# Attention and a gated feed-forward on one core: row sums moved to other slots, feed-forward from an earlier pair, and feed-forward steps in 32-column tiles

## The chip, the core and the metric

The kernel runs on one core of a Trainium2 chip. The core has a matrix engine (TensorE, PE in the profile, its weight loads PEld), a vector engine (VectorE, DVE), an engine for functions such as exp and tanh (ScalarE, ACT), a general engine (GpSimd, POOL) and a queue engine (SyncE, SP), which work side by side and wait for each other by semaphores. DMA engines move data between main memory (HBM) and the on-chip memory SBUF. TensorE writes its results to a second on-chip memory, PSUM, from which VectorE or ScalarE must fetch them.

The metric is the device time of one execution, in microseconds. Before the change it is 474.34 us (median of three runs, 473.15 to 475.47).

## The reference

```python
# q, k, v: (8, 12, 448, 64) float32       batch, heads, sequence, head size
scores = matmul(q, k^T) / sqrt(64)
attn   = exp(scores - max(scores)); attn = attn / (sum(attn) + 1e-9)
x      = matmul(attn, v)                  # then heads side by side: (3584, 768)
g      = x @ w_gate                       # (768, 1536)
val    = x @ w_val                        # (768, 1536)
out    = (g * sigmoid(g) * val) @ w_out   # (1536, 768) -> (3584, 768) float32
```

So there is attention for 96 heads, and then a gated feed-forward block over the 3,584 tokens. The kernel leaves out the subtraction of the maximum, because the scores are small, and works in 16-bit floats with sums in 32 bits.

## The kernel before

Heads are taken two at a time: 48 pairs, six to a batch. The main loop has one slot for each pair. Each slot has two halves, and in each half TensorE makes half of the pair's scores, which ScalarE turns into exponentials E.

```python
    def qk_half(pr, half):
        ...
        for c in (2 * half, 2 * half + 1):
            s = ps_s.tile([128, 2, 512], FP32, tag="s")          # two buffers
            for hx in range(2):
                nc.tensor.matmul(s[:, hx, 0:S], lhsT=t[ts(hx, 64)]..., rhs=t[ts(hx, 64), NC:, :]..., ...)
            nc.scalar.activation(E[pr][:, c], s[0:P, :, 0:S], AF.Exp, scale=sm_scale)
```

The two matmuls of a chunk use 64 rows of the array each. The product with V ("PV") uses four column tiles of 32 columns, and so do the row sums of E, which two pairs share. PV is copied out of PSUM by VectorE.

```python
    def pv(pr):
        acc = ps_a.tile([128, 512], FP32, tag="acc")             # one buffer
        for c in range(NC):
            for j in range(4):
                nc.tensor.matmul(acc[ts(j, 32), 0:S], lhsT=vt[:, 2 * r + j // 2, c, ts(j % 2, 32)],
                                 rhs=E[pr][:, c, j // 2, :], ...)
        xr = attp.tile([128, S], FP32, tag="xraw")
        nc.vector.tensor_copy(xr[:], acc[:, 0:S])

    def sum_rows(p0, acc):
        for c in range(NC):
            for j in range(4):
                nc.tensor.matmul(acc[ts(j, 32), 0:S], lhsT=ones[:], rhs=E[p0 + j // 2][:, c, j % 2, :], ...)
```

For batch 0 the reciprocal sums are spread over the 64 rows of each head by a float32 matmul with a selector matrix, and VectorE multiplies PV with them into X, the input of the feed-forward. For later batches DMAs spread them instead, and GpSimd multiplies.

```python
    def sums_pe(p0, pieces):
        acc = ps_f.tile([128, 512], FP32, tag="f")
        sum_rows(p0, acc)
        R = attp.tile([128, S], FP32, tag="R", bufs=2)
        for lo, hi in pieces:
            nc.vector.reciprocal(R[:, lo:hi], acc[:, lo:hi])

        def spread():
            for lo, hi in pieces:
                for u in range(2):
                    rb = ps_f.tile([128, 512], FP32, tag="f", name="rb")
                    nc.tensor.matmul(rb[:, lo:hi], lhsT=sel[:, u, :], rhs=R[:, lo:hi], start=True, stop=True)
                    mult(p0 + u, nc.vector, rb, lo, hi)
        return spread
```

The feed-forward is cut into steps: the gate (gp), the value (vp) and the output (op). Each step is a group of 6 or 12 matmuls of 128 rows by 128 columns.

```python
    def ffn1_steps(kk, c0, n, hts):
        for fb in range(NFB):
            gp = ps_f.tile([128, 512], FP32, tag="f")            # three buffers for f
            for cb in range(NCB):
                nc.tensor.matmul(gp[:, 0:n], lhsT=wslice("g", fb, cb), rhs=X[kk][:, cb, ds(c0, n)], ...)
            ...  # tanh on ScalarE, then vp in the same way, two operations on VectorE
```

The main loop, cut to the order in which a slot issues its work; steps of the feed-forward fill both halves of a slot, up to a budget that spreads a block evenly over the slots until the next one:

```python
        wp = ps_f.tile([128, 512], FP32, tag="f", name="wp")
        for _ in range(7):
            nc.tensor.matmul(wp[:], lhsT=warm[:, 0:128], rhs=warm[:], start=True, stop=True)
        ...
        for pr in range(NPAIR + 1):
            ...
            if pr == NHP:                      # pair 6: end of batch 0
                pv(pr - 1)
                spread = sums_pe(pr - 2, ((0, 192), (192, S)))
            if pr < NPAIR:
                qk_half(pr, 0)
            if pr == 0:
                turn()                         # transposes of pair 1
            ...
            if pr >= 1 and pr != NHP:
                pv(pr - 1)
            if pr > NHP and pr % 2 == 0:
                work, mults = sums(pr - 2)
                ...
            if pr in add_at:                   # from pair FIRST = 7
                add_block(add_at[pr])
            ...
            carry = ffn_run(state["left"] / slots + carry)
            if pr < NPAIR:
                qk_half(pr, 1)
            if turn2:
                turn2()                        # transposes of pair pr + 2
            if pr in (3, 5, 6):
                spread()
            if pr in (2, 4):
                spread = sums_pe(pr - 2, ((0, S),))
            ...
            carry = ffn_run(state["left"] / max(1, slots - 1) + carry)
```

Of the kernel before, what the change touches and what calls it, by code (L numbers as in the profile page):

```python
# [10 lines left out]
FP32 = mybir.dt.float32  # L11
# [7 lines left out]
GP = 3  # L19
NPE = 11  # L20
LA = 6
FIRST = 7


@with_exitstack
def kernel(
# [10 lines left out]
    nc = tc.nc  # L37
    B, H, S, D = q.shape
# [6 lines left out]
    NHP = H // 2  # L45
# [9 lines left out]
            name=nc.get_next_instruction_name(),  # L55
# [132 lines left out]
    def pv(pr):  # L188
        g, r = divmod(pr, GP)
        vt = v16[g]  # L190
        acc = ps_a.tile([128, 512], FP32, tag="acc")
        for c in range(NC):
            for j in range(4):
                nc.tensor.matmul(  # L194
                    acc[ts(j, 32), 0:S],
                    lhsT=vt[:, 2 * r + j // 2, c, ts(j % 2, 32)],
                    rhs=E[pr][:, c, j // 2, :],
                    start=(c == 0),
                    stop=(c == NC - 1),
                )  # L200
        xr = attp.tile([128, S], FP32, tag="xraw")
        nc.vector.tensor_copy(xr[:], acc[:, 0:S])  # L202
        xraw[pr] = xr

    def mult(pr, eng, rb, lo=0, hi=S):
# [19 lines left out]
# [4 lines that stand above are left out]
        for lo, hi in pieces:  # L229
            nc.vector.reciprocal(R[:, lo:hi], acc[:, lo:hi])  # L230

        def spread():
            for lo, hi in pieces:
                for u in range(2):
                    rb = ps_f.tile([128, 512], FP32, tag="f", name="rb")
                    nc.tensor.matmul(  # L236
                        rb[:, lo:hi], lhsT=sel[:, u, :], rhs=R[:, lo:hi], start=True, stop=True
                    )
                    mult(p0 + u, nc.vector, rb, lo, hi)

        return spread

    def sums(p0):
# [18 lines left out]
        work.append(bcast)  # L262
        return work, [lambda u=u: mult(p0 + u, nc.gpsimd, Rb[p0 + u]) for u in range(2)]

    def ffn1_steps(kk, c0, n, hts):
        for fb in range(NFB):
            gp = ps_f.tile([128, 512], FP32, tag="f")
            for cb in range(NCB):
                nc.tensor.matmul(  # L269
                    gp[:, 0:n],  # L270
                    lhsT=wslice("g", fb, cb),
                    rhs=X[kk][:, cb, ds(c0, n)],
                    start=(cb == 0),
                    stop=(cb == NCB - 1),
                )
            sg = fp.tile([128, 512], FP32, tag="sg")
            nc.scalar.activation(sg[:, 0:n], gp[:, 0:n], AF.Tanh, scale=0.5)  # L277
            yield NCB * n / 2400.0
            vp = ps_f.tile([128, 512], FP32, tag="f")
            for cb in range(NCB):  # L280
                nc.tensor.matmul(  # L281
                    vp[:, 0:n],
                    lhsT=wslice("v", fb, cb),
                    rhs=X[kk][:, cb, ds(c0, n)],
                    start=(cb == 0),
                    stop=(cb == NCB - 1),
                )
            t1 = fp.tile([128, 512], FP32, tag="t1")
            nc.vector.scalar_tensor_tensor(  # L289
                t1[:, 0:n], sg[:, 0:n], 1.0, gp[:, 0:n], ALU.add, ALU.mult  # L290
            )
            nc.vector.scalar_tensor_tensor(  # L292
                hts[:, fb, 0:n], t1[:, 0:n], 0.5 * HS, vp[:, 0:n], ALU.mult, ALU.mult
            )
            yield NCB * n / 2400.0

    def ffn2_steps(kk, c0, n, hts, last_block):
        for ch in range(n // 128):
            osb = fp.tile([128, DM], FP32, tag="osb", bufs=2)
            for oh in range(2):  # L300
                if last_block and ch == n // 128 - 1 and oh == 1:
                    osb = fp.tile([128, DM], FP32, tag="osb", bufs=2)
                op = ps_f.tile([128, 512], FP32, tag="f")
                for fb in range(NFB):
                    nc.tensor.matmul(  # L305
                        op[:, 0:OH],
                        lhsT=hts[:, fb, ts(ch, 128)],
                        rhs=wo[fb // (NFB // 3)][:, fb % (NFB // 3), ts(oh, OH)],
                        start=(fb == 0),
                        stop=(fb == NFB - 1),  # L310
                    )
                last = last_block and ch == n // 128 - 1
                if last and oh == 1:
                    m = OH // 2
                    nc.scalar.activation(
                        osb[:, OH : OH + m], op[:, 0:m], AF.Copy, scale=1.0 / HS
                    )
                    nc.vector.tensor_scalar_mul(osb[:, OH + m : DM], op[:, m:OH], 1.0 / HS)
                else:
                    nc.scalar.activation(osb[:, ts(oh, OH)], op[:, 0:OH], AF.Copy, scale=1.0 / HS)  # L320
                if oh == 1 or last:
                    m0, m1 = (oh * OH, oh * OH + OH) if last else (0, DM)
                    l0 = c0 + ch * 128
                    l = l0
                    while l < l0 + 128:
                        b, j = divmod(l, S)
                        c, p0 = divmod(j, P)
                        m = min(P - p0, l0 + 128 - l)
                        eng = nc.scalar if last and m < 64 else nc.sync
                        eng.dma_start(  # L330
                            out[ts(NB * kk + b, S), :].rearrange("(p c) m -> c p m", c=NC)[
                                c, p0 : p0 + m, m0:m1
                            ],
                            osb[l - l0 : l - l0 + m, m0:m1],
                        )
                        l += m
                yield NFB * OH / 2400.0
# [7 lines left out]
    with tc.manual_schedule():  # L345
# [13 lines left out]
        load_qk16(3, 1)  # L359
        load_qk16(4)  # L360
        load_v(1)
        wp = ps_f.tile([128, 512], FP32, tag="f", name="wp")
        for _ in range(7):
            nc.tensor.matmul(wp[:], lhsT=warm[:, 0:128], rhs=warm[:], start=True, stop=True)
        prep(0)()
        turn = prep(1)

# [11 lines left out]
        def emit(item):  # L379
            if item[0] == "qk":  # L380
                load_qk16(*item[1:])
            elif item[0] == "V":
                load_v(item[1])
            else:
                load_w(*item)
# [49 lines left out]
        add_at = {FIRST: 0}  # L435
        for i in range(1, B - 1):
            add_at[NHP * (i + 1) + DELAY] = i
        for pr in range(NPAIR + 1):
            if pr in add_at:
                pop_deferred(99)  # L440
            nxt = min([x for x in add_at if x > pr] + [NPAIR + 4])
            slots = 2 * (nxt - pr)
            turn2 = None
            if NPE <= pr + LA < NPAIR:
                load_qk(pr + LA, touch=pr < 9)
            if pr == NHP:
                pv(pr - 1)
                spread = sums_pe(pr - 2, ((0, 192), (192, S)))
            if pr < NPAIR:
                qk_half(pr, 0)  # L450
            if pr == 0:
                turn()
            if pr + 3 < NPAIR and pr + 3 >= NPE:
                prep(pr + 3)
            if pr + 2 < NPAIR:
                if pr + 2 < NPE:
                    turn2 = prep(pr + 2)
                if (pr + 2) % GP == GP - 1 and 4 <= (pr + 2) // GP + 1 < NGRP:
                    load_v((pr + 2) // GP + 1)
            if pr >= 1 and pr != NHP:  # L460
                pv(pr - 1)
            if pr > NHP and pr % 2 == 0:
                work, mults = sums(pr - 2)
                deferred.extend(work)
                held[pr + 1] = mults
            if pr in add_at:
                add_block(add_at[pr])
            for w in wq.pop(pr, []):
                emit(w)
            carry = ffn_run(state["left"] / slots + carry)  # L470
            if pr < NPAIR:
                qk_half(pr, 1)
            if turn2:
                turn2()
            if pr in (3, 5, 6):
                spread()
            if pr in (2, 4):
                spread = sums_pe(pr - 2, ((0, S),))
            for fn in held.pop(pr, []):
                deferred.append(fn)  # L480
            if not backlog:
                pop_deferred(7)
            carry = ffn_run(state["left"] / max(1, slots - 1) + carry)
        for fns in held.values():
            deferred.extend(fns)
        ffn_run(1e9)
# [35 lines left out]
```

The softmax here doesn't subtract the row's maximum and nothing guards it: scores larger than these inputs give would overflow.

## Time and profile before

| what | value |
|---|---|
| time, median of three | 474.34 us |
| span of the profiled execution | 473.3 us |
| exponentials on ScalarE | 192 of 915 ns, 164.4 us busy |
| gate, value and output matmuls | 576 + 576 + 672 |
| PV and row-sum matmuls | 768 + 384 |
| granted TensorE clock, mean | 0.991 |

A line of the profile's groups names the line of the kernel, the engine, the operation, what is written and read, the tile, and how often. The matmuls on TensorE are pipelined: the profile's length of a matmul includes its way through the array, and the next one starts well before that ends. So what a group costs is read from the start of one group to the start of the next.

### The profile page before, as it was taken

The numbers are of one execution on the slowest core, as the hardware profiler recorded it, in microseconds if no ns is written. First come the engines' busy times: TensorE is split into PE (matmuls) and PEld (weight loads), VectorE is DVE, ScalarE is ACT, GpSimd is POOL, SyncE is SP. The second block draws the span as 40 slices with busy tenths as digits, with TensorE's granted clock in tenths as the row PEclk, the third lists the DMA queues.
The fourth block names the chain that finished last, engine by engine and source line by source line (L and its number), as shares of the span: only waits on it lengthen the run. The fifth ranks groups of instructions, "written<-read, shape, count | busy, mean of one in ns | idle before, by whom it ended". The sixth has DMA issues, their size and how long they took to land.

```text
span 473.3 us, 8811 instructions
## 1 busy us (share of the span) xinstructions
PE 461.7 (98%) x3559; PEld 219.4 (46%) x3559; DVE 245.3 (52%) x383; ACT 237.4 (50%) x345; POOL 120.8 (26%) x164
## 2 busy tenths in 40 slices
PE   7989999999999999999999999999999999999996
PEld 3335444433345545444444554444444445554453
DVE  3676775077665644636555545456365456334310
ACT  5765665555555465454455465455545552222221
POOL 9534032522443044030340340330401111000000
PEclk8999999999999999999999999999999999999999
DMA  9999999986966595645847668754743312201123
GB/s 142 196 209 239 200 231 187 255 167 117 186 150 133 113 194 135 122 110 125 173 100 160 150 155 136 162 118 93 139 87 67 72 40 73 67 1 34 35 66 101
DMA packets 86025, 62.03 MB, mean 131 GB/s; under 512 B 38496, under 2 KB 82528, under 8 KB 85984
## 3 DMA queue, kind: packets, MB, share of 16 engines
q1 hardware_dynamic: 63872, 46.53, 43.3%
q0 software_dynamic: 22048, 14.88, 22.3%
q8 instruction: 28, 0.46, 0.4%
q14 instruction: 13, 0.11, 0.1%
q10 hardware_dynamic: 64, 0.05, 0.0%
HBM read 47.19 MB, written 11.01 MB: 123 GB/s over the span
## 4 chain that ended last, share of the span: by engine, by line
PE 91%; ACT 3%; DMA 3%; issue 1%; SPq 0%; DVE 0%; POOL 0%; ACTq 0%; POOLq 0%
PE gp L269 24%; PE vp L281 24%; PE op L305 21%; PE s L179 9%; PE acc L194 8%; PE acc L217 4%; ACT E L186 3%; PE rb L236 1%; DMA out_dram<-osb 1%; PE tp L164 1%; DMA Rb<-R 1%; DMA rk<-in_k_dram 1%; SPq L153 0%; POOL qk L150 0%; POOL X L210 0%
## 5 line engine op out<-in xcount | busy, mean ns | idle before, releaser
L186 ACT ACTIVATE E<-s 112x896 f16<-112x896 f32 x192 | 164.4, 915 | 33.2 <-PE s L179 33.2
L269 PE MATMUL gp<-X,wg 128*128 128x384 f16 (+1 forms) x576 | 125.1, 353 | 0.0
L281 PE MATMUL vp<-X,wv 128*128 128x384 f16 (+1 forms) x576 | 124.9, 353 | 0.0
L305 PE MATMUL op<-wo,hts 128*128 128x384 f16 x672 | 117.0, 326 | 0.0
L210 POOL TENSOR_TENSOR X<-xr,Rb 128x448 f16<-128x448 f32 x42 | 47.6, 1133 | 259.7 <-DMA Rb<-R 258.5
L277 ACT ACTIVATE sg<-gp 128x384 f32<-128x384 f32 (+1 forms) x96 | 52.3, 544 | 103.1 <-PE gp L269 103.0
L289 DVE SCALAR_TENSOR_TENSOR t<-sg,gp 128x384 f32<-128x384 f32 (+1 forms) x96 | 58.8, 612 | 83.2 <-ACT sg L277 82.5
L305 PEld LDWEIGHTS <-hts 128*128 128x128 f16 x672 | 64.8, 98 | 48.3 <-issue 4.5
L281 PEld LDWEIGHTS <-wv 128*128 128x128 f16 x576 | 54.3, 98 | 57.1 <-issue 8.9
L269 PEld LDWEIGHTS <-wg 128*128 128x128 f16 x576 | 52.6, 98 | 60.3 <-issue 16.7
L292 DVE SCALAR_TENSOR_TENSOR hts<-t,vp 128x384 f16<-128x384 f32 (+1 forms) x96 | 59.6, 621 | 29.8 <-PE vp L281 22.2
L320 ACT ACTIVATE osb<-op 128x384 f32<-128x384 f32 x55 | 27.0, 491 | 93.7 <-PE op L305 90.6
L202 DVE COPY xr<-acc 128x448 f32<-128x448 f32 x48 | 29.7, 619 | 80.8 <-PE acc L194 79.6
L251 DVE RECIPROCAL R<-ssb 128x112 f32<-128x112 f32 x84 | 66.9, 828 | 0.7
L179 PE MATMUL s<-qkT 64*128 64x448 f16 x384 | 55.6, 361 | 5.6 <-ACT E L186 4.4
L194 PE MATMUL acc<-E,vt 112*32 112x448 f16 x768 | 45.9, 360 | 0.0
L179 PEld LDWEIGHTS <-qkT 64*128 64x128 f16 x384 | 12.3, 94 | 41.4 <-issue 37.8
L194 PEld LDWEIGHTS <-vt 112*32 112x32 f16 x768 | 16.3, 96 | 26.0 <-issue 18.3
L150 POOL CAST qk<-rk 112x512 f16<-112x512 f32 x37 | 22.7, 614 | 0.0
L150 POOL CAST qk<-rq 112x512 f16<-112x512 f32 x37 | 22.7, 613 | 0.0
L217 PE MATMUL acc<-E,ones 112*32 112x448 f16 x384 | 22.4, 353 | 0.0
L126 POOL DMA_DIRECT2D vt<-in_v_dram x17 | 13.5, 792 | 2.4 <-DMA wg<-in_moe_w_gate_dram 2.4
(37 smaller groups left out, 94.1 us busy)
## 6 DMA issues: line engine op xcount, KB each, us to landing
Rb<-R SPq DMA_DIRECT2D x84, 112.0 KB, 2.3
rq<-in_q_dram SPq DMA_DIRECT2D x38, 224.0 KB, 3.7
rk<-in_k_dram SPq DMA_DIRECT2D x38, 224.0 KB, 3.9
vt<-in_v_dram POOLq DMA_DIRECT2D x15, 336.0 KB, 6.2
out_dram<-osb SPq DMA_DIRECT2D x7, 336.0 KB, 3.0
wg<-in_moe_w_gate_dram POOLq DMA_DIRECT2D x4, 576.0 KB, 17.6
wv<-in_moe_w_val_dram POOLq DMA_DIRECT2D x4, 576.0 KB, 19.4
wo<-in_moe_w_out_dram POOLq DMA_DIRECT2D x3, 768.0 KB, 28.3
```

The costliest lines, as they stand in the source:

```text
L150: eng.tensor_copy(qk16[:, 1 - t].rearrange("p c h d -> p h c d"), src[:])
L179: nc.tensor.matmul(s[:, hx, 0:S], lhsT=t[ts(hx, 64)].rearrange("p c q -> p (c q)")[:, c * P : c * P + 128], rhs=t[ts(hx, 64), NC:, :].rear ...
L186: nc.scalar.activation(E[pr][:, c], s[0:P, :, 0:S], AF.Exp, scale=sm_scale)
L194: nc.tensor.matmul(acc[ts(j, 32), 0:S], lhsT=vt[:, 2 * r + j // 2, c, ts(j % 2, 32)], rhs=E[pr][:, c, j // 2, :], start=(c == 0), stop=(c ...
L210: eng.tensor_tensor(X[kk][:, hp, bb * S + lo : bb * S + hi], xraw[pr][:, lo:hi], rb[:, lo:hi], ALU.mult)
L251: work.append(lambda i=i: nc.vector.reciprocal(R[:, ts(i, P)], ssb[:, ts(i, P)]))
L269: nc.tensor.matmul(gp[:, 0:n], lhsT=wslice("g", fb, cb), rhs=X[kk][:, cb, ds(c0, n)], start=(cb == 0), stop=(cb == NCB - 1),)
L277: nc.scalar.activation(sg[:, 0:n], gp[:, 0:n], AF.Tanh, scale=0.5)
L281: nc.tensor.matmul(vp[:, 0:n], lhsT=wslice("v", fb, cb), rhs=X[kk][:, cb, ds(c0, n)], start=(cb == 0), stop=(cb == NCB - 1),)
L289: nc.vector.scalar_tensor_tensor(t1[:, 0:n], sg[:, 0:n], 1.0, gp[:, 0:n], ALU.add, ALU.mult)
L292: nc.vector.scalar_tensor_tensor(hts[:, fb, 0:n], t1[:, 0:n], 0.5 * HS, vp[:, 0:n], ALU.mult, ALU.mult)
L305: nc.tensor.matmul(op[:, 0:OH], lhsT=hts[:, fb, ts(ch, 128)], rhs=wo[fb // (NFB // 3)][:, fb % (NFB // 3), ts(oh, OH)], start=(fb == 0), s ...
```

## The change: what it does and what it is for

It has three parts.

1. The row sums of batch 0 move from the end of slots 2 and 4 to their first half, right behind PV, which has the same tile shape. The selector matmuls, which ran two at a time at the end of slots 3 and 5, are spread: one each at the end of slots 3, 4 and 5 and one in slot 6, and the last two pairs' are cut at column 384, which is where the first feed-forward block ends. PV of pair 5 is copied out by ScalarE. Four dummy matmuls are added in slot 0. This is to keep every half-slot of TensorE short enough for ScalarE never to lack scores, and to keep TensorE's clock up.
2. The first block of the feed-forward begins in the second half of slot 6 rather than in slot 7.
3. From pair 14 on, the feed-forward steps in the first half of a slot, which follow PV or the row sums, are issued as four matmuls of 32 columns each in place of one of 128. Their tile shape is then that of PV. The results are the same.

```diff
-FIRST = 7
+FIRST = 6
+TILED = 14
...
-        nc.vector.tensor_copy(xr[:], acc[:, 0:S])
+        if pr == NHP - 1:
+            nc.scalar.copy(xr[:], acc[:, 0:S])
+        else:
+            nc.vector.tensor_copy(xr[:], acc[:, 0:S])
...
-        def spread():
-            for lo, hi in pieces:
-                for u in range(2):
+        def spread(us=(0, 1), parts=pieces):
+            for lo, hi in parts:
+                for u in us:
...
+    tiled = [False]
+
+    def mm(dst, lhsT, rhs, start, stop):
+        if not tiled[0]:
+            nc.tensor.matmul(dst, lhsT=lhsT, rhs=rhs, start=start, stop=stop)
+            return
+        for j in range(4):
+            nc.tensor.matmul(
+                dst[ts(j, 32), :], lhsT=lhsT[:, ts(j, 32)], rhs=rhs, start=start, stop=stop
+            )
...                                     # gp, vp and op alike:
-                nc.tensor.matmul(
+                mm(
                     gp[:, 0:n],
...
-        wp = ps_f.tile([128, 512], FP32, tag="f", name="wp")
-        for _ in range(7):
-            nc.tensor.matmul(wp[:], lhsT=warm[:, 0:128], rhs=warm[:], start=True, stop=True)
+
+        def dummy(n):
+            wp = ps_f.tile([128, 512], FP32, tag="f", name="wp")
+            for _ in range(n):
+                nc.tensor.matmul(wp[:], lhsT=warm[:, 0:128], rhs=warm[:], start=True, stop=True)
+
+        dummy(7)
...
             if pr == NHP:
                 pv(pr - 1)
-                spread = sums_pe(pr - 2, ((0, 192), (192, S)))
+                first, rest = (0, 384), (384, S)
+                spread = sums_pe(pr - 2, (first, rest))
             if pr < NPAIR:
                 qk_half(pr, 0)
             if pr == 0:
+                dummy(1)
                 turn()
+                dummy(1)
...
             if pr >= 1 and pr != NHP:
                 pv(pr - 1)
+            if pr in (2, 4):
+                spread = sums_pe(pr - 2, ((0, S),))
+            if pr == NHP:
+                spread23((1,))
+                spread(parts=(first,))
...
-            if pr in add_at:
+            if pr in add_at and pr != FIRST:
                 add_block(add_at[pr])
             for w in wq.pop(pr, []):
                 emit(w)
+            tiled[0] = pr >= TILED
             carry = ffn_run(state["left"] / slots + carry)
+            tiled[0] = False
             if pr < NPAIR:
                 qk_half(pr, 1)
+            if pr == 0:
+                dummy(2)
             if turn2:
                 turn2()
-            if pr in (3, 5, 6):
-                spread()
-            if pr in (2, 4):
-                spread = sums_pe(pr - 2, ((0, S),))
+            if pr in (3, 4):
+                spread01((pr - 3,))
+            if pr == 5:
+                spread23((0,))
+            if pr == 2:
+                spread01 = spread
+            if pr == 4:
+                spread23 = spread
+            if pr == FIRST:
+                add_block(0)
+                slots -= 1
...
             carry = ffn_run(state["left"] / max(1, slots - 1) + carry)
+            if pr == FIRST:
+                spread(parts=(rest,))
```

## The prediction

> **What bounds the kernel now.** I read the page's busy times first, then the waits of TensorE, then its instructions in order of time, because a busy TensorE says little until one knows how closely its matmuls follow each other.
>
> ```profile
> PE 461.7 (98%) x3559; PEld 219.4 (46%) x3559; DVE 245.3 (52%) x383; ACT 237.4 (50%) x345; POOL 120.8 (26%) x164
> ```
>
> TensorE is busy for 98% of the span and no other engine for more than 52%. The table by stretches (length, then each engine's busy time and count, then TensorE's clock, the share of the DMA engines, GB/s) shows where the missing 2% and the slow clock lie:
>
> ```profile
> 4.00:7.30 3.30, 2.05 (x37) 1.22 (x37) 1.60 (x5) 0.82 (x2) 3.30 (x6) 1.00 1.11 125
> 7.40:14.10 6.70, 6.41 (x62) 2.64 (x62) 1.70 (x4) 5.44 (x7) 6.45 (x9) 0.50 1.34 172
> 14.20:40.00 25.80, 22.81 (x288) 10.32 (x286) 19.59 (x27) 18.53 (x23) 8.33 (x12) 1.00 1.31 211
> 94.00:400.00 306.00, 306.00 (x2335) 141.47 (x2324) 171.55 (x263) 163.13 (x237) 81.15 (x107) 1.00 0.61 127
> ```
>
> From 94 us on TensorE never stops, so there only fewer or tighter TensorE instructions help. In the first 40 us it waits, and from 7.4 to 14.1 us it has half its clock. Two regimes, so two sums.
>
> In the long regime, the timeline of TensorE (start, length with the pipeline's tail, group):
>
> ```profile
> 202.32 0.94 PE L194 MATMUL acc<-E,vt 112*32 112x448 f16 x16
> 203.19 1.47 PE L269 MATMUL gp<-X,wg 128*128 128x512 f16 x6
> 204.50 1.46 PE L281 MATMUL vp<-X,wv 128*128 128x512 f16 x6
> 205.79 1.46 PE L269 MATMUL gp<-X,wg 128*128 128x512 f16 x6
> 207.19 0.55 PE L179 MATMUL s<-qkT 64*128 64x448 f16 x4
> ...
> 211.50 0.94 PE L194 MATMUL acc<-E,vt 112*32 112x448 f16 x16
> 212.27 0.93 PE L217 MATMUL acc<-E,ones 112*32 112x448 f16 x16
> 213.13 1.47 PE L269 MATMUL gp<-X,wg 128*128 128x512 f16 x6
> ```
>
> I take starts, not lengths. PV (16 matmuls of 32 columns) followed by the row sums, also of 32 columns, takes 212.27-211.50 = 0.77 us; followed by a full 128-column step it takes 203.19-202.32 = 0.87. The first full step takes 1.31, the second 1.29, and one ahead of the 64-row score matmuls (s) 207.19-205.79 = 1.40. So each change of tile shape costs about 0.10 us, and a new shape's first step 0.01 to 0.02 more.
>
> The early regime is a chain between TensorE and ScalarE. ScalarE's timeline there:
>
> ```profile
> 6.48 3.34 ACT L186 ACTIVATE E<-s 112x896 f16<-112x896 f32 x4 [4.46 <-PE s L179]
> 10.32 1.72 ACT L186 ACTIVATE E<-s 112x896 f16<-112x896 f32 x2 [0.51 <-PE s L179]
> 12.79 5.07 ACT L186 ACTIVATE E<-s 112x896 f16<-112x896 f32 x6 [0.75 <-PE s L179]
> 18.36 3.34 ACT L186 ACTIVATE E<-s 112x896 f16<-112x896 f32 x4 [0.50 <-PE s L179]
> 23.20 3.34 ACT L186 ACTIVATE E<-s 112x896 f16<-112x896 f32 x4 [1.49 <-PE s L179]
> 27.12 3.34 ACT L186 ACTIVATE E<-s 112x896 f16<-112x896 f32 x4 [0.58 <-PE s L179]
> 33.58 3.34 ACT L186 ACTIVATE E<-s 112x896 f16<-112x896 f32 x4 [3.13 <-PE s L179]
> ```
>
> Four exponentials make a pair, at a pitch of (5.07-0.92)/5 = 0.83 us. Before pair 6 ScalarE stands idle 0.51+0.75+0.50+1.49+0.58+3.13 = 6.96 us, always for scores, because a half-slot of TensorE carries row sums or both selector matmuls on top of the rest; while in others TensorE waits for ScalarE. The first feed-forward step starts at 39.38.
>
> **The Trainium skill.** "TensorEngine Tiling (Array Packing)", Key Properties, says that changing the tiling mode, not just the tile, drains TensorE; the 0.10 us above agree. The same page, Gotcha 2: Feature Incompatibilities, says that column tiling excludes Fast Weight Load, which would speak against 32-column steps; in this trace it costs nothing visible, since the weight loads of PV take 96 ns on average against 98 for the feed-forward's and lie beside matmuls. "TensorE: Matmul & The Clock Gate", Part 3 (The mechanism), says that matmuls on different tiles overlap; PV agrees: 16 matmuls of 448 columns in 0.77 us are 0.19 per four, about one 448-column stream. The same page's Part 1 (What's actually happening) says the clock is gated by how busy TensorE was in a window of about 3.4 us that doesn't start with the kernel; the stretch at 0.50 of clock after a stretch that was 2.05/3.30 = 62% busy fits.
>
> **The change, part by part.**
>
> *32-column steps.* From pair 14 the feed-forward steps of a slot's first half, which follow PV or the sums, are issued as four 32-column matmuls in place of one. In the built order of instructions these are 606 of the 1,824 feed-forward matmuls, hence 1,818 more matmuls and as many weight loads. Cost of the stream: PV's four take 0.19 us at 448 columns; a 128-column matmul takes 1.29/6 = 0.2155 at 512 columns, times 448/512 = 0.189. The same, so the stream costs 0 within what the timeline resolves. Shortest case: 384 columns, 0.975/6 = 0.1625 us per group of four; PV's weight loads of 97 ns fit beside it. What goes is one change of shape per slot: PV-to-step 0.10, first-step 0.01; step-to-scores stays (0.10 either way: sums to scores take 17.89-17.02 = 0.87, against 0.77 without a change). Slots 14 to 47 are 34, and slot 48 only moves its change. 34 x 0.105 = 3.6 us, all on the path.
>
> *Early slots.* Units from the timelines: scores of a half-slot 0.48 us, PV 0.87, sums 0.86, transposes 0.51, one selector matmul pair 1.70/2 = 0.85, exponentials at 0.83, scores to exponential 0.46, reciprocal of 448 columns 2.96. Assume the four extra dummy matmuls keep the clock at full. Two come before pair 0's second scores, which wait for ScalarE anyway; two (0.43 plus changes) fall at 8.6 to 9.1, where TensorE waits for pair 2's data until 8.74. Pair 1 starts its exponentials at about 10.15 (before 10.32) but then never lacks scores: they end at 13.5, where before the next pair's began at 14.5. In pair 2 PV and sums now stand ahead of the second scores: 13.8+0.77+0.86 = 15.4, plus 0.46, so ScalarE idles 0.7 and goes on to 17.5. Pair 3 (one selector) runs 17.5 to 20.85. In pair 4 two small gaps, 0.45 after the selector and 0.4 after the sums: 21.3 to 25.1. Pair 5 from 25.3 to 28.65. PV of pair 5 and sums then end at 30.5; scores of pair 6 follow, exponential at 30.9 (before 33.58). Now the new wait: the reciprocal of columns 0 to 384 takes 2.54 us, from 30.76 to 33.3, and the 384-column selector matmuls stand in TensorE's order ahead of the second scores. TensorE does pair 3's selector until 31.95 and idles to 33.4; two selectors, 0.75 each, to 34.95; scores 35.5; transposes 36.0; feed-forward from about 36.1.
>
> That is 3.3 us sooner, but the work done by then differs: still owed are one half of scores 0.48, one PV 0.87 and the 64-column selectors about 0.35; one transpose group 0.51 is done in advance. 3.3-0.48-0.87-0.35+0.51 = 2.1 us gained. Without the full clock I put about 1.0 less: the gain at pair 1 goes and the dummies cost double. I weigh the two roughly equally: 1.6.
>
> *The rest.* The amount of feed-forward is the same; starting it half a slot after pair 6's first scores only fills waits. Block 0 spread over 15 half-slots in place of 14 leaves the three waits on ScalarE between 74 and 92 us (1.5 us) of the same kind. PV's copy of pair 5 on ScalarE costs it some 0.55, counted above. The tail is untouched.
>
> Sum: 474.3 - 3.6 - 1.6 = 469.1, say 469.2.
>
> **Rivals.** (1) The 32-column steps stream more slowly when kept up: four weight loads and four matmuls each 160 ns at 128 rows, not 190 at 112. For it: nothing in this trace holds that pace for more than 32 matmuls but the transposes, which do 16 in 0.39 us. Those, at 25 ns per matmul and load, speak against it. Each 10 ns per group would cost 6 us: 475. (2) The supply of instructions: TensorE's list grows by half and in the tiled half-slots it asks for some 48 per us. The sums right after PV already take 64 in 1.63 us without a gap. If it stalled once per slot for 0.3 us, +10: 480. (3) The early gain is eaten: the DMA share is over 1.3 until 14 us, so inputs for pairs 3 to 5 may land no sooner, the clock may stay low, and the wait for the reciprocal is real. Then only the 3.6 remain, or less: 471 to 472. (4) The early regime tightens more than I count; of the 6.96 us idle on ScalarE, 2 more would give 467.
>
> **Range and chances.** The two sums give 469 to 471; rivals 3 and 4 give 467 to 472; the three times before lie 2.3 us apart. Eight in ten: 466.8 to 472.8. Two per cent faster would be under 464.9, which needs the whole early idle time back; two per cent slower is over 483.8, which needs rival 1 or 2 in force.
>
> **What would show it.** Tiled steps: four-matmul groups at 0.1625 and 0.2155 us, PV followed by a tiled step after 0.77, no idle TensorE in 94 to 400 us. Sums in the early slots: pair 6's first exponential near 30.9, feed-forward from about 36.1, TensorE idle about 1.5 us ahead of the 384-column selectors. Clock: 1.00 in 7.4 to 14.1. The prediction is wrong if a tiled group is longer than a full matmul, if TensorE shows waits for its own issue there, or if the first feed-forward step starts after 38.

## The result: 0.6% faster, 471.53 us

The changed kernel takes 471.53 us (median of four runs, 470.86 to 471.93), the kernel before 474.69 beside it. The ratio is 0.9936, 95% interval 0.9907 to 0.9965: 3.0 us less, where 5.1 were foretold.

The profiled pair differs by more, 473.3 against 468.7 us of span, so that pair is read first and the times decide. The page of the changed kernel has the same bound as before:

```profile
PE 456.8 (97%) x5381; PEld 227.0 (48%) x5381; DVE 243.6 (52%) x382; ACT 238.8 (51%) x346; POOL 121.4 (26%) x164
```

TensorE has 1,822 matmuls more and is busy for 4.9 us less. The table by stretches (length, then busy time and count of each engine, TensorE's clock, share of the DMA engines, GB/s):

```profile
4.00:7.30 3.30, 2.33 (x39) 1.27 (x38) 1.21 (x3) 0.95 (x2) 3.30 (x6) 1.00 1.09 123
7.40:14.10 6.70, 5.92 (x79) 2.51 (x82) 2.47 (x4) 6.47 (x8) 6.09 (x9) 1.00 1.31 163
14.20:40.00 25.80, 23.29 (x286) 10.83 (x282) 18.95 (x26) 18.09 (x24) 9.02 (x12) 1.00 1.31 214
94.00:400.00 306.00, 305.31 (x4145) 151.96 (x4141) 170.50 (x263) 164.31 (x239) 84.16 (x109) 1.00 0.62 129
```

Here the clock is whole from 7.4 to 14.1, where it was half. From 94 us on TensorE is busy all the time but for 0.69 us at the very beginning of the stretch. The timeline of TensorE in a slot with 32-column steps:

```profile
200.00 0.94 PE L195 MATMUL acc<-E,vt 112*32 112x448 f16 x16
200.77 1.47 PE L276 MATMUL gp<-X,wg 128*32 128x512 f16 x24
202.06 1.47 PE L276 MATMUL vp<-X,wv 128*32 128x512 f16 x24
203.36 1.47 PE L276 MATMUL gp<-X,wg 128*32 128x512 f16 x24
204.76 0.55 PE L180 MATMUL s<-qkT 64*128 64x448 f16 x4
```

PV to the first step takes 0.77 us, where it took 0.87. The 24 small matmuls of a step take 1.29 to 1.30 us, as six large ones did, and the last one ahead of the scores 1.40. ScalarE's timeline in the early slots:

```profile
6.35 3.37 ACT L187 ACTIVATE E<-s 112x896 f16<-112x896 f32 x4 [4.33 <-PE s L180]
9.88 5.13 ACT L187 ACTIVATE E<-s 112x896 f16<-112x896 f32 x6 [0.16 <-PE s L180]
15.60 5.07 ACT L187 ACTIVATE E<-s 112x896 f16<-112x896 f32 x6 [0.59 <-PE s L180]
21.21 1.73 ACT L187 ACTIVATE E<-s 112x896 f16<-112x896 f32 x2 [0.54 <-PE s L180]
23.27 1.73 ACT L187 ACTIVATE E<-s 112x896 f16<-112x896 f32 x2 [0.33 <-PE s L180]
25.27 3.34 ACT L187 ACTIVATE E<-s 112x896 f16<-112x896 f32 x4 [0.28 <-PE s L180]
29.80 0.53 ACT L204 COPY xr<-acc 128x448 f32<-128x448 f32 x1 [1.19 <-PE acc L195]
30.90 1.73 ACT L187 ACTIVATE E<-s 112x896 f16<-112x896 f32 x2 [0.57 <-PE s L180]
```

Pair 6 begins at 30.90, the number of the prediction; it was 33.58. The first feed-forward step starts at 35.66, where 36.1 was foretold. So both parts do what they were to do, and yet something takes time back. The table of TensorE's waits names it:

```profile
PE gp L276 <- POOL X L214: 2.4, 2, 1.7
PE s L180 <- ACT E L187: 1.7, 5, 0.4
PE rb L240 <- DVE R L234: 1.2, 1, 1.2
```

The third line is the wait for the reciprocal ahead of the 384-column selectors, which the prediction had. The first is new: the first step of the second feed-forward block (block 1) waits for GpSimd to multiply X of pairs 10 and 11, the last two of batch 1. In the kernel before, the same place looks like this in the timeline:

```profile
94.75 1.47 PE L269 MATMUL gp<-X,wg 128*128 128x512 f16 x6
96.15 0.55 PE L179 MATMUL s<-qkT 64*128 64x448 f16 x4
```

and in the changed kernel:

```profile
90.92 1.04 PE L276 MATMUL gp<-X,wg 128*32 128x512 f16 x16
93.67 0.40 PE L276 MATMUL gp<-X,wg 128*32 128x512 f16 x4 [1.71 <-POOL X L214]
94.76 0.40 PE L276 MATMUL gp<-X,wg 128*32 128x512 f16 x4 [0.69 <-POOL X L214]
95.09 0.55 PE L180 MATMUL s<-qkT 64*128 64x448 f16 x4
```

Counted by starts: block 1 begins 3.83 us sooner (94.75 against 90.92), of which 1.9 come from the early slots and 1.9 from three waits for ScalarE between 76 and 93 us that are gone. Then the step takes 4.17 us in place of 1.40. So 2.77 of the 3.83 are given back, and the next scores are 1.06 us ahead. The rest of the 4.6 us between the two spans, 3.5, comes after that, in 33 slots with a change of shape less.

Only half of the 2.77 us comes from being early. These are GpSimd's multiplications of X for pairs 10 and 11, in the kernel before and then in the changed one:

```profile
91.24 2.22 POOL L210 TENSOR_TENSOR X<-xr,Rb 128x448 f16<-128x448 f32 x2 [5.85 <-DMA Rb<-R]
```

```profile
92.50 2.21 POOL L214 TENSOR_TENSOR X<-xr,Rb 128x448 f16<-128x448 f32 x2 [7.70 <-DMA Rb<-R]
```

Before, X of pair 11 is ready at 93.46, and the step needs it in its last matmul, at about 95.8 (five matmuls of 0.2155 us behind 94.75). That is a slack of 2.4 us, and block 1 was pulled forward by 3.83: 1.4 us of wait. The other 1.3 arise because X is now ready 1.25 us later, at 94.71, although the row sums ahead of it start 0.5 us sooner (77.50 against 78.00). The list of DMA issues from 84 to 94 us has the reason: the four DMAs that spread the reciprocals (Rb) take 4.0 us to land before (median), and 6.0 in the changed kernel.

```profile
Rb<-R SPq DMA_DIRECT2D x4, 112.0 KB, 4.0
```

```profile
Rb<-R SPq DMA_DIRECT2D x4, 112.0 KB, 6.0
```

Why they land later is not shown. The last two of the three waits for ScalarE in the kernel before go back to a transfer too: ahead of the exponentials, ScalarE's copy of an output waits for an output DMA.

```profile
90.67 0.49 ACT L320 ACTIVATE osb<-op 128x384 f32<-128x384 f32 x1 [3.05 <-DMA out_dram<-osb]
```

### The profile page after: what moved, and what is told of

Read it like the earlier page. It is cut to its first block, busy times and chain, and to the rows that moved or that the text cites. A ratio compares the mean times of both kernels' runs of the same rounds, so it can differ in the third digit from the quotient of the medians.

```text
span 468.7 us, 12457 instructions
## 1 busy us (share of the span) xinstructions
PE 456.8 (97%) x5381; PEld 227.0 (48%) x5381; DVE 243.6 (52%) x382; ACT 238.8 (51%) x346; POOL 121.4 (26%) x164
## 3 DMA queue, kind: packets, MB, share of 16 engines
q1 hardware_dynamic: 63872, 46.53, 44.3%
## 4 chain that ended last, share of the span: by engine, by line
PE 92%; DMA 3%; POOL 1%; ACT 1%; DVE 1%; issue 1%; SPq 0%; POOLq 0%; ACTq 0%
PE op L273 19%; PE vp L273 15%; PE gp L276 12%; PE gp L273 12%; PE s L180 9%; PE vp L276 9%; PE acc L195 8%; PE acc L221 4%; PE op L276 3%; DMA Rb<-R 1%; ACT E L187 1%; DMA k<-in_k_dram 1%; PE rb L240 1%; PE tp L165 1%; DVE R L234 1%
## 5 line engine op out<-in xcount | busy, mean ns | idle before, releaser
L273 PE MATMUL op<-wo,hts 128*128 128x384 f16 x576 | 100.1, 326 | 0.0
L273 PE MATMUL vp<-X,wv 128*128 128x512 f16 (+1 forms) x360 | 78.4, 354 | 0.0
L273 PEld LDWEIGHTS <-hts 128*128 128x128 f16 x576 | 55.2, 98 | 42.5 <-issue 5.1
L276 PE MATMUL gp<-X,wg 128*32 128x512 f16 (+1 forms) x1176 | 65.3, 355 | 2.4 <-POOL X L214 2.4
L273 PE MATMUL gp<-X,wg 128*128 128x384 f16 (+1 forms) x282 | 60.4, 350 | 0.0
L273 PEld LDWEIGHTS <-wv 128*128 128x128 f16 x360 | 33.7, 98 | 36.2 <-issue 6.7
L276 PE MATMUL vp<-X,wv 128*32 128x384 f16 (+1 forms) x864 | 46.8, 351 | 0.0
L276 PEld LDWEIGHTS <-wg 128*32 128x32 f16 x1176 | 31.6, 97 | 27.6 <-issue 3.0
L273 PEld LDWEIGHTS <-wg 128*128 128x128 f16 x282 | 26.2, 98 | 27.2 <-issue 5.6
L276 PEld LDWEIGHTS <-wv 128*32 128x32 f16 x864 | 23.2, 97 | 17.4
```

The lines of the kernel that those rows point to most:

```text
L273: nc.tensor.matmul(dst, lhsT=lhsT, rhs=rhs, start=start, stop=stop)
L276: nc.tensor.matmul(dst[ts(j, 32), :], lhsT=lhsT[:, ts(j, 32)], rhs=rhs, start=start, stop=stop)
```

## The experiments

The question is what each part is worth, whether the change of shape is the cause, and what the wait at block 1 costs. All ratios are to the kernel before on the same chip. "Span" is the mean over a kernel's runs, from first to last instruction, less that of the kernel before on that chip.

| run | time, us | ratio (95%) | span, us |
|---|---|---|---|
| 32-column steps alone | 470.98 | 0.9917 (0.9889 to 0.9946) | -4.0 |
| all but the 32-column steps | 474.74 | 0.9988 (0.9977 to 1.0000) | -0.9 |
| without dummies | 470.90 | 0.9918 (0.9890 to 0.9946) | -4.3 |
| block 1 later | 471.74 | 0.9925 (0.9901 to 0.9949) | -4.0 |
| changed kernel again | 471.36 | 0.9944 (0.9930 to 0.9957) | -2.9 |
| spreading DMAs first | 472.13 | 0.9954 (0.9937 to 0.9971) | -2.4 |
| all steps tiled | 472.03 | 0.9955 (0.9939 to 0.9970) | -2.2 |
| 54 changes of shape more | 480.41 | 1.0141 (1.0122 to 1.0160) | +6.8 |
| feed-forward from slot 7 | 470.88 | 0.9926 (0.9902 to 0.9951) | -4.0 |
| copy of pair 5 on VectorE | 471.50 | 0.9939 (0.9918 to 0.9960) | -3.3 |
| selectors for pairs 10, 11 | 470.91 | 0.9923 (0.9900 to 0.9947) | -3.8 |
| four edits together | 470.86 | 0.9916 (0.9893 to 0.9939) | -4.0 |

Most intervals are 1 us wide to each side or more. Differences of 1 us between two of these kernels are not resolved. Against the kernel before, all differences in the table are, but for the 0.6 us of the second row.

**Each part alone.** The first kernel is that of before with the tiles:

```diff
+TILED = 14
...
+            tiled[0] = pr >= TILED
             carry = ffn_run(state["left"] / slots + carry)
+            tiled[0] = False
```

> The kernel before with the 32-column steps alone, from pair 14. Theory: one change of tile shape less in each of 34 slots, 0.107 us each, so 3.6 us less than before (ratio 0.992), PV to first step 0.77 us, groups of four at the pitch of one full matmul, and no wait of TensorE for X at the start of block 1, because nothing before slot 14 moves. Rival (instruction supply or weight loads too slow): 2 us less or nothing, with TensorE idle inside tiled groups.

Measured: ratio 0.9917, 3.9 us less, with no wait for X. The second is the changed kernel with `TILED = 99`, so without tiles.

> The changed kernel without the 32-column steps. Theory: by the starts of groups the early slots give 1.9 us and three waits for ScalarE before block 1 (1.9 us) go away, but 2.8 us are lost at the start of block 1, where TensorE waits for X of pairs 10 and 11. So about 1.0 us less than before (ratio 0.998), with a wait of some 2.3 us near 91 us. Rival (the early slots carry the whole gain of the change): 3 to 4.6 us less.

Measured: 0.9988, 0.6 us less, with up to 1.1 less and none at all both inside its interval (22 runs). Its waits for X at 91 us are there (1.4 us in the table of waits, 1.7 by starts). So the 32-column steps carry the gain, and the early slots, the larger part of the diff, bring at most 1.1 us. If both simply added up, the changed kernel would be 4.5 us faster; its two measurements and that of the kernel which differs only in the copy of pair 5 (on VectorE) say 2.6 to 3.0. A part of that lies within the intervals; what else it is comes below.

**Is it the change of shape?** If so, more changes must cost in proportion. In the kernel before, the steps of a first half, from slot 14 on, now alternate between 128 and 32 columns, beginning with 128:

```diff
                 gen, t = backlog.pop(0)
+                if first[0]:
+                    tiled[0] = not tiled[0]
                 next(gen)
...
+            first[0] = pr >= TILED
+            tiled[0] = first[0]
             carry = ffn_run(state["left"] / slots + carry)
+            first[0] = tiled[0] = False
```

> The kernel before with tile shapes alternating inside the first half of each slot from 14 on: first step 128 columns, second 32, third 128. Same streams, but 54 more changes of shape than before. Theory: 0.105 us for each, so 5.7 us more than before (ratio 1.012). Rival (what the change saves is not the change of shape but something of the 32-column steps themselves): the same as before, or less.

Measured: 1.0141, 6.7 us more, 0.124 us for each of the 54 changes. The timeline of TensorE in one of those slots shows where:

```profile
205.07 1.47 PE L271 MATMUL gp<-X,wg 128*128 128x512 f16 x6
206.47 1.48 PE L274 MATMUL vp<-X,wv 128*32 128x512 f16 x24
207.88 1.47 PE L271 MATMUL gp<-X,wg 128*128 128x512 f16 x6
209.28 0.55 PE L180 MATMUL s<-qkT 64*128 64x448 f16 x4
```

Every step takes 1.40 or 1.41, against 1.29 without a change behind it. It matters not whether it has large tiles or small ones. That is the cause, shown from both sides: 34 changes fewer give 3.9 us, 54 more cost 6.7.

The traces give a tighter size than the times, because they leave out what happens before block 1. From the scores behind block 1's first step to the end of the span, the kernel before takes 473.3-96.15 = 377.15 us and that without tiles 377.17. The changed kernel takes 373.61 and 373.75 in its two profiles, the 32-column steps alone 373.70. With 54 changes more it is 383.16. So 33 changes fewer give 3.4 to 3.5 us and 54 more cost 6.0: 0.10 to 0.11 us for each. What the times have beyond that is their scatter.

**Do small tiles cost anything when they are many?** The changed kernel, with the line `tiled[0] = False` taken out, so that every feed-forward step from slot 14 on is tiled:

> The changed kernel with every feed-forward step from slot 14 to the end in 32-column tiles, also those in second halves and in the tail: some 3,000 more matmuls and weight loads. Theory: a group of four streams exactly as one full matmul and the change of shape against the scores is there in any case, so the same time as the changed kernel within 0.5 us. Rival (supply of instructions, or weight loads that no longer hide): each group 5 to 10 ns longer, 5 to 10 us more, with idle time inside groups.

Measured: 0.9955 against 0.9944 for the changed kernel on the same chip, 0.5 us more, with 3,006 matmuls more. TensorE in the long stretch (all 290 us of it, 5,836 matmuls):

```profile
110.00:400.00 290.00, 290.00 (x5836) 150.38 (x5828) 161.54 (x249) 154.73 (x226) 78.19 (x102) 1.00 0.65 125
```

There is no idle time, and no slower pitch either: at 303.57 us a step of 24 takes 1.30 us to the start of the next. Rivals 1 and 2 of the prediction fall. One single stall of that kind was seen in any of the traces (TensorE's waits, in the kernel with the spreading DMAs first):

```profile
PE gp L273 <- issue: 0.9, 1, 0.9
```

The same kernel with all steps tiled shows what the wait at block 1 can bring with it:

```profile
93.00:95.90 2.90, 1.21 (x12) 0.31 (x11) 0.00 (x0) 0.36 (x1) 2.90 (x4) 1.00 1.25 93
96.10:99.40 3.30, 3.30 (x36) 1.36 (x32) 1.44 (x3) 1.65 (x3) 1.93 (x4) 0.50 1.14 358
```

TensorE was busy for 1.21 of 2.90 us, and right behind that the clock is halved for 3.4 us, which costs 1.8 us more in two steps (2.46 us and 1.93 by starts in place of 1.30). The trace without dummies has the same after its wait, and from there to the end it takes 375.33 us in place of the 373.7 above. In both traces of the changed kernel the clock stays whole. With the copy on VectorE, three of eleven runs have a mean clock of 0.996, which is what 3.4 us at half make of 470; their spans are 471.0 to 471.7, the mean of the other eight 469.1. But the clock also falls at the end of a trace, where TensorE has no work left (at 468.3 of 468.7 us in the changed kernel), and that lowers the mean at no cost. So it is not shown that these three lost it at block 1.

**The dummies.**

```diff
             if pr == 0:
-                dummy(1)
                 turn()
-                dummy(1)
...
-            if pr == 0:
-                dummy(2)
```

> The changed kernel without its four dummy matmuls in slot 0. Theory: the clock falls to half from about 7 to 14 us as in the kernel before; PV, scores and transposes take twice as long there, ScalarE lacks scores again, and the first feed-forward step starts about 1.0 us later than 35.66; the order of all that follows is fixed, so the end is 1.0 us later too. Rival (the moved row sums alone keep the clock up, the dummies only cost): clock 1.00, 0.3 to 0.5 us sooner.

In this profile the mechanism is right; the price isn't. The clock falls at 8.0 us and returns at 14.8, and the feed-forward begins at 37.23 in place of 35.66. But the time, 0.9918, is no worse than that of the changed kernel. Half of the delay is taken up at block 1: it is 1.57 us at the first feed-forward step and 0.78 at the scores behind block 1's first step (95.87 against 95.09). Also, the dummies don't always help: in three of the profiles with them TensorE starts slow. Its timeline in the changed kernel's second profile, and then in the first, for the same scores:

```profile
6.43 0.93 PE L180 MATMUL s<-qkT 64*128 64x448 f16 x4 [0.49 <-DVE qkT L169]
```

```profile
5.94 0.55 PE L180 MATMUL s<-qkT 64*128 64x448 f16 x4 [0.48 <-DVE qkT L169]
```

In the second profile the clock rises at 10.53, and the feed-forward starts at 37.54, 1.9 us later than in the first.

**The wait at block 1.** Four kernels try to be rid of it. First, in the order of steps: block 1 begins in the second half of slot 14 (the second entry of `LATE`), and block 0 is spread over one half-slot more.

```diff
+        LATE = (FIRST, min(x for x in add_at if x > FIRST))
...
-            slots = 2 * (nxt - pr)
+            slots = 2 * (nxt - pr) + (nxt == LATE[1])
...
-            if pr == FIRST:
-                add_block(0)
+            if pr in LATE:
+                pop_deferred(99)
+                add_block(add_at[pr])
                 slots -= 1
```

> The changed kernel with the second feed-forward block begun half a slot later (second half of slot 14 rather than first) and the first block spread over one more half-slot. Theory: the wait of TensorE for X of pairs 10 and 11 (2.8 us by the starts) is only a matter of order; with attention work ahead of it the wait goes and the end comes 2.4 to 2.8 us sooner than in the changed kernel. Rival (the wait is bandwidth of the DMA engines or GpSimd, which then delays the next thing): less than 1 us sooner, with a wait elsewhere between 85 and 105 us.

The wait for X is gone from the list, but the time is not: 0.9925. In the profile TensorE loses 1.3 us to ScalarE between 89.8 and 92.4 us instead, and 0.5 at 75.4 us, where it waits for a transposing DMA; the feed-forward also began at 36.72 in it. ScalarE in turn stands behind an output DMA there: its copy at 89.95 waits 1.75 us for one. So the rival is right, about the sum and about the DMA engines.

Second, in the queue. The four DMAs that spread the reciprocals (Rb) were issued late; the queue of SyncE in the changed kernel:

```profile
82.88 1.22 SPq L154 DMA_TRANSPOSE qkT<-qk  x1
84.20 1.03 SPq L345 DMA_DIRECT2D out_dram<-osb  x2
85.32 2.76 SPq L262 DMA_DIRECT2D Rb<-R  x4
```

The reciprocals were finished at 82.14 (four at 79.15, 2.99 us in all), but the DMAs stand behind a transpose and two output DMAs.

```diff
                 work, mults = sums(pr - 2)
-                deferred.extend(work)
+                if pr == 2 * NHP:
+                    for fn in work:
+                        fn()
+                else:
+                    deferred.extend(work)
```

> The changed kernel with the reciprocals and the four spreading DMAs of pairs 10 and 11 issued directly behind their row sums, ahead of the output DMAs and transposes in the queue of SyncE. Theory: these DMAs were held at 85.3 us by that queue although the reciprocals were done at 82.1; now they start near 82.2, X is ready about 3 us sooner, TensorE's wait at block 1 falls from 2.9 us to under 0.5, and the end comes about 2.4 us sooner than in the changed kernel. Rival (the DMA engines are full with the last weights and the spread lands no sooner): under 1 us, the DMAs take longer to land.

They start at 85.17, where the changed kernel on the same chip has 86.88: a transpose, which waits for GpSimd, is still ahead of them. And they take longer to land: 7.1 us from issue to landing (median of the four) against 5.7, so that X's multiplication begins at 93.25 against 93.65. The time is 0.9954. The theory that the queue is the cause falls, and the rival's forecast is borne out, though not its reason: the last DMA of weights was issued at 44.3 us and none took longer than 27.7. What else is issued between 84 and 94 us are inputs, outputs and transposes. Over all 84 the same DMAs land in 2.3 us (median); from 85 to 95 us the share of the DMA engines is 1.25 here.

Third, without those DMAs: the selectors of batch 0 for pairs 10 and 11.

```diff
+            if pr == 2 * NHP:
+                spread1 = sums_pe(pr - 2, ((0, S),))
+            if pr == 2 * NHP + 1:
+                spread1()
-            if pr > NHP and pr % 2 == 0:
+            if pr > NHP and pr % 2 == 0 and pr != 2 * NHP:
```

> The changed kernel with the reciprocal sums of pairs 10 and 11 spread by the selector matmuls of batch 0 in place of DMAs. Theory: the wait of 2.1 to 2.9 us at block 1 is the time that the spreading DMAs take to land among the other transfers; without them it goes, for 1.9 us more of TensorE (two selector matmuls and changes of shape). So the span is 0.2 to 1.0 us shorter than the changed kernel's, and the start of block 1 shows no wait over 0.3 us. Rival (X is late for another reason): the wait stays and the end is 1 to 2 us later.

Block 1 now runs without any wait in TensorE's timeline:

```profile
92.69 0.93 PE L221 MATMUL acc<-E,ones 112*32 112x448 f16 x16
93.45 1.47 PE L276 MATMUL gp<-X,wg 128*32 128x512 f16 x24
94.86 0.55 PE L180 MATMUL s<-qkT 64*128 64x448 f16 x4
```

That TensorE comes here later than in the changed kernel (93.45 against 90.92) isn't the reason: VectorE has multiplied X of these pairs by 87.7. So the spread by DMA, with GpSimd's multiplication behind it, was the cause of the wait. The selectors cost 1.6 us (from 85.25 to 86.86) in a place where TensorE had work, and most of the wait is paid for in that way: span 0.5 us less than the kernel with the copy on VectorE on the same chip, which is inside both spreads.

Fourth, the start of the feed-forward in slot 7 again (`FIRST = 7`, and the 64-column selectors at the end of slot 6):

> The changed kernel with the feed-forward started in slot 7 again, row sums, selectors and dummies as changed. Theory: TensorE comes to block 1 with more of block 0 behind it in the same slots, so what slot 6 no longer takes comes back as a shorter wait for X at block 1 (2.1 to 2.9 us in the changed kernel, under 1.5 here); the end within 0.7 us of the changed kernel. Rival (starting in slot 6 is worth its two steps): 1.5 to 2 us more than the changed kernel, with the same wait.

0.9926: no slower than with slot 6. Starting half a slot after the scores of pair 6 is worth nothing that could be measured. The waits stand elsewhere again, as the timeline of TensorE shows:

```profile
87.92 2.12 PE L273 MATMUL op<-wo,hts 128*128 128x384 f16 x12
90.64 0.36 PE L180 MATMUL s<-qkT 64*128 64x448 f16 x2 [0.60 <-ACT E L187]
91.45 0.37 PE L180 MATMUL s<-qkT 64*128 64x448 f16 x2 [0.44 <-ACT E L187]
93.27 1.47 PE L276 MATMUL gp<-X,wg 128*32 128x512 f16 x24
```

These are the waits for ScalarE of the kernel before, and the same transfer stands behind them: ScalarE's copy at 89.29 us waits 3.06 us for an output DMA. Block 1 starts at 93.27 and then doesn't wait, so that what came back was not a shorter wait for X, as expected, but those for ScalarE in its place.

**Controls.** The changed kernel once more, on the chip of the three kernels beside it:

> The changed kernel itself once more, on the same chip as the three kernels beside it. Both theories: 3 us less than the kernel before (ratio 0.9935), spans near 469.3, a wait of 2 to 3 us for X at the start of block 1.

0.9944, so 2.65 us, with a wait of 2.0 us by starts. The last question is small. In this kernel, and in each of those with the changed early slots and DMAs for pairs 10 and 11, the time is on average 2.12 to 2.18 us longer than the span; in the kernel before, in that with tiles alone and in that with more changes 1.76 to 1.82. So 0.3 us of what the span gains doesn't reach the time.

> The changed kernel with PV of pair 5 copied by VectorE again. In all kernels with the changed early slots the time exceeds the span by 2.15 us, in the others by 1.8. Theory: the copy on ScalarE is what they share, so the excess falls to 1.8 and the time by 0.35 us; the span stays within 0.3 us, since VectorE's copy lies ahead of the end of the row sums. Rival: the excess stays 2.15 us and comes from something else in the early slots.

With the copy back on VectorE it is 2.14: not the copy. The kernel with selectors for pairs 10 and 11, which keeps ScalarE's copy, has 1.80. Why, is open.

**Four edits together.** Selectors for pairs 10 and 11, the copy on VectorE, tiles from slot 6, and the second scores of slot 6 ahead of the 384-column selectors:

> The changed kernel with four edits: selectors for pairs 10 and 11 as in the run beside it, the copy of pair 5 on VectorE, 32-column steps from slot 6 on, and the second scores of slot 6 ahead of the 384-column selectors. Theory: 0.2 to 1.0 for the wait, 0.35 for the copy, 7 slots of 0.107 = 0.75 for the changes of shape, 0.5 for the idle time ahead of the selectors: 1.8 to 2.6 us less than the changed kernel, ratio to before 0.989. Rival (what is gained before block 1 is lost in waits there): within 0.7 us of the changed kernel.

0.9916, 4.0 us less than before, which is also what the 32-column steps give alone (0.9917). Against the changed kernel that is 0.9 to 1.3 us less, under what was expected, and hardly resolved. The wait for the reciprocal and the wait for X are both gone from its trace; that profile, though, started with the slow clock, so that its early slots can't be compared one to one.

## Why the prediction was right in range and too high in gain

*32-column steps:* right in cause and nearly in size. PV to step 0.77, equal pitch, the change against the scores kept. Predicted 3.6, measured alone 3.9 (2.6 to 5.3). The times of the opposite experiment make 0.124 of a change, where 0.105 had been read; the traces behind block 1 make 0.10 to 0.11. Rivals 1 and 2 were rightly given little.

*Early slots:* the ledger held step by step: exponentials at 9.88 (10.15), pair 6 at 30.90 (30.9), feed-forward at 35.66 (36.1), an idle TensorE of 1.2 us ahead of the selectors (1.5). By the first two slots of the feed-forward the profiled pair had gained 1.9 us (2.1). That the two agree is in part luck. The sum of 2.1 credits 0.51 for transposes done in advance, but both kernels have done those of pair 8 by the first feed-forward step (35.65 before, 35.14 after). Without the credit it is 1.6, and what made up for it is that the step came 0.44 us sooner than foretold. Nor did ScalarE lack scores "always" because of row sums or selectors: its first two waits, of 0.51 and 0.75 us, fall into the stretch at half clock, with neither ahead of them. Measured as time, all of the early slots together is 0.6.

*The step that failed* is in "The rest": that starting sooner "only fills waits" and that block 0 in 15 half-slots leaves the waits for ScalarE "of the same kind". They went, and block 1 came 3.83 us sooner to an X that was not ready. The end of a batch is a second deadline in this kernel: block 1 can't finish its first step before the last sums of batch 1 are made, inverted, spread by DMA and multiplied. That chain started 0.5 us sooner, but ended 1.25 us later. With the 2.4 us of slack that the kernel before had, this gives 2.7 of the 2.77 us that were lost. The prediction had looked for such a wait in slot 6 alone and has no term for X at block 1. Rival 3, that the early gain is eaten, was the one that came true, in another place: not at the inputs of pairs 3 to 5 but at X of pairs 10 and 11.

*The clock:* the dummies hold it in most profiles, as assumed. About 1.0 us was put on that, with an even chance; one profile without them shows 1.6 us at the first feed-forward step. In time it doesn't show. Half of it is taken up at block 1, and the rest is below what the runs resolve.

What stays open: 1.5 to 1.9 us between the sum of the two parts (4.5) and the changed kernel (2.6 to 3.0), or 1.1 to 1.5 with the 3.5 us that the traces give for the tiles. The intervals allow most of it. The 0.3 us beyond the span don't explain it, since the kernel without tiles has them too. The half clock after the wait is a candidate: two profiles show it, at 1.6 to 1.8 us, but neither of those of the changed kernel.

## What to carry to other kernels

Look at which tile shapes stand next to each other on TensorE: where a column-tiled group is followed by full matmuls, issuing those as four column tiles removes a change of shape, here, at 384 to 512 columns, at no cost in stream. When work is pulled forward past one wait, follow it to the next point where it needs data from another chain; a point without a wait may have little slack. Read that slack from the trace before, and remember that the other chain can move as well. A gain ahead of such a meeting point was worth little here, and shortening the other chain cost most of the wait.

## What the runs showed of the hardware that I had not expected

- A change of tile shape costs 0.10 to 0.11 us of TensorE in each order that could be read: from 32-column tiles to full matmuls (0.77 to 0.87 us), from full ones to 32-column tiles (1.29 to 1.40), and from either to 64-row scores (1.30 to 1.40).
- Changes of the clock lie whole multiples of 3.41 us apart in every trace: half clock lasts from 7.34 to 14.16 us in the kernel before, and from 96.02 to 99.43 with all steps tiled. How busy TensorE was in such a window doesn't by itself decide what follows. In the second full window of the kernel, 2.03 to 2.14 us (the three kernels without dummies whose clock came early) lost the clock, and 2.29 to 2.75 (seven profiles with dummies) kept it. But 2.18 us from 31.35 and 1.84 us from 92.79, in the changed kernel, kept it as well, where 1.81 us from 93.34, without dummies, lost it. And 3.06 us at half clock, from 7.34 in the kernel before, were followed by another window at half.
- When the full clock comes first goes with where these windows lie against the start of the kernel, which differs from run to run. It came at 3.9 to 5.6 us in ten profiles, whose windows, counted back, begin 0.45 to 2.16 us after the start. It came at 10.3 to 12.8 us in four, with windows at 0.01 to 0.29 or 2.37 to 2.58. The column of the clock shows 1.00 ahead of its first record, also where the scores took 0.93 us in place of 0.55; the durations tell the truth there.
- A wait of two to three microseconds in the middle of a kernel can be followed by 3.4 us at half clock, and so cost 1.6 to 1.8 us beyond its length. After the waits of the changed kernel, 2.8 and 2.0 us long, that didn't happen.
